# A half chunk of keys in four quarters of the array: head-mixed attention in front of two gated layers

## The chip, the cores and the metric

The kernel runs on one core of one Trainium2 chip. The metric is the time of the device in microseconds (us) for one execution; a time that is given for a kernel is the median of several runs. The profile is of one execution, taken by the hardware profiler, and has its own time.

## The reference

Attention with 4 batches, 12 heads, 448 positions and 64 numbers a head, in which the heads are mixed before and after the softmax, and behind it two gated layers:

```python
scores = scale * np.matmul(q, k.transpose(0, 1, 3, 2))
scores = np.einsum('bhij,hg->bgij', scores, w_pre)      # first mixing
scores = scores - np.max(scores, axis=-1, keepdims=True)
attn = np.exp(scores)
attn = attn / (np.sum(attn, axis=-1, keepdims=True) + 1e-09)
attn = np.einsum('bhij,hg->bgij', attn, w_post)         # second mixing
out = np.matmul(attn, v)
...
gate = 1.0 / (1.0 + np.exp(-(x @ w_gate)))              # 1792 x 768, d_ff 1536
x = gate * (x @ w_val) @ w_out
h = x @ w_in                                            # d_ff 2048
return h * (1.0 / (1.0 + np.exp(-1.702 * h))) @ w_out2
```

All of it is float32.

## The kernel before, in words

The program has two parts. `attention` does the attention and writes its result to `xd` in memory; `Ffn` does the two layers from `xd`. The change touches `attention` and one helper of `Ffn` (`prepare`) that works beside it.

In `attention` the 448 queries of a batch are cut into four units of 120, 120, 120 and 88 queries, 16 units in all. For each of the six pairs of heads of a batch, q and k are loaded as rows (`load_pair`, tile `nat`), turned on TensorE against an identity (`turn`, L300: four transposes of 112 rows for a part, k and q apart; q of the first batch comes in two halves), and copied into `kq` by ScalarE or VectorE. `qk` (L340) makes the scores of a unit. A DMA per half group (`relayout`, `gt<-sc`, L359) puts five queries x twelve heads on 60 partitions; two such blocks lie in the two row halves of the array. A unit of 120 queries has 6 groups of 20 queries, one of 88 has 2 of 20 and 3 of 16: 92 groups. Per group come `premix` (L368, the first mixing, in four quarters of 64 x 64 of the array), maximum and exponent, `norm` (its last step on GpSimd, L393, makes `w`, the second mixing's weights divided by the sums) and `postmix` (L415, the second mixing).

The 448 keys are seven chunks of 64. `postmix` lays chunk c on partitions 0 to 63 and chunk c + 4 on 64 to 127 of its result. The fourth chunk has no partner: its two matmuls per row half both go to the left column half, and the other 64 partitions hold zeros. `post_out` copies the result to `at`; `av` (L436) multiplies it with v: for each of 12 heads 4 matmuls over all 128 partitions, two heads abreast in the two column halves. The fourth of the four is half zeros: `vt[64:, :, NC - 1]` is set to 0 once. A float32 matmul is two records in the trace, so a group of `postmix` has 56 records (28 matmuls) and a unit of `av` 96 (48 matmuls). `vt` is one buffer: `load_v` (L326) brings v of the next batch in two large DMAs once the last `av` of the batch has read it.

The order on every engine is written out: each piece of work is added to a list with the engines it may use, and `PLAN` is a text of tokens, one per piece, that fixes the order in which pieces are issued, their engine (S for ScalarE, V for VectorE, P for GpSimd, Y for SyncE) and their PSUM banks. Each engine works its pieces off in that order and waits for what a piece needs. SyncE issues nearly all DMAs. Beside the attention run 28 pieces of weight conversion for `Ffn` (`prepare`: a load into `pf`, steps on ScalarE and VectorE, a write of `pc` to `kept`), load and write on SyncE.

Of the kernel before, what the change touches and what calls it, by code (L numbers as in the profile page):

```python
# [9 lines left out]
F32 = mybir.dt.float32  # L10
# [64 lines left out]
0Y 3:0 1S 6:1 7V 1cY cS 1f:2 f:3 1oY 8 oS pS dY 4V 5 20:45 10S 11Y gV h r:6 sV 1gS 1h 1dS 1pS 2Y qY 21S u:7 vV  # L75
t i:1 eY jS k w 13:0 1r:3 16:2 14S 17V 22V 1i:6 1jS 23:41 1sS 1k 2c:75 15 25S 12S 24V 9:6 aS 18 2eS 1u:1 29:04
1t 1vV 1w 2dS 2bS 26:23 28S 1qY 2f:51 2aV 27V dd de 19:7 l:0 1x:4 2gS 2hV mV 1aV 1b b 4z:32 51V df:5 x:1 yV
1eS n dgV dh 1yS 1z 58:76 5aV 52:20 59S 54S 5e:75 2i 2j 2k:04 2l 53S 2v 50S di:2 2w 38 39 5gS 2n 3l 3m 3y 3z
4b 5fS z 2x:63 2y 2m 1l:5 1mV 1n 2z 2o 55:70 56S 4c 1fg 30 5b:15 5dV 3a:64 3b djS dk 31 32 2p 3c 3n:75 3d 3e
5cS 3f 2q 33 34 2r 57S 40:32 41 42 3o 3g 3h 3p 2s:64 3q 43 2tV 3r 3i:10 44 45 4d:37 4e 2uS 4g 4o 3jV 3kV 4f 4h  # L80
4i 4j 5h 7w:56 7yV 46 3s 5i 7xS 35:24 36S 3t 82:31 dl 7z:70 80V 37V 83S 84S 4k 88:56 89S 5u 85:23 87V 4l:17 3u
81V 3v:45 4mV 3wS 4nV 3xS 5j:30 47 48:17 5k 4p 5v 5m 86S 8b:45 49S 4aV 5l 5n 5w:21 4q:7 8cV 5x 5y 1fw 4r 67 68
5o 6k 5p 5q 8aV 4s dn:3 1fx 5z 60 69:40 4u:2 4v 6l 6x 6y 7a 7b 1fh 4w 8dV dt 5r:65 61 4tV 1fy 1fz 6a 8e 6b 6c
6d doS 6m:17 4xS dp 62 5sS 5tS 1g0 6z:40 7c:32 8f 8r 8s 6n 6p 6e 6o 6q 63 70 6f 71 72 73 1g2 at:65 avS auV
64:17 7d 7e 74 6g 94 6h:46 6r 6iS 7f 7g 6jV 8g:05 95 dv:3 dm 6s 6t 65S b2:46 66S dwV 8h 6u:21 7h 7i 9h 1g1 9i
8i 6vS az:70 b3V 7j 1g3 b1S dx 8j 7k:43 8k 75 76 e9 6wV aw:21 7lV du 7mS b0S 8t:05 1g4 1g5 8u q2 axS ayS 1g6
eh b4S dq:4 77:37 drS 96:21 97 9u 9v 1g8 8v 9j:60 9k e1 78S 79S 7n:3 a7 8l 7o 7p 9l 8w 8x 98 99 b8:76 9a b5:52
a8 9b e2 b6S dy:1 9m ds b9V 9n 9c 9o baV ea eb:4 ecS 8m b7V 8n dzS e0 ed 1g9 1ga 9w:75 7r:6 7s 7t 9x 9z 9y 7qV
q3 8y 8z ei qa 7uS ej:0 bb bc 9d e3:2 ekV a9:14 a0 bo a1 8o:73 1gb 1gc 90 e4S 8pS q4:6 a2 1ge 8qS 9p e6:5 1g7
ee:7 efS aa el 9e:03 1fi ab q5S e7V e8 9q 9fS em:5 enS e5 ep:12 eg 9gV ac ev:70 eqS q6 exS eo 4yP ad ae qc:3  # L90
bp q7:1 9r:60 ewS af qi qdV erS 9sS 9tV a3 a4:54 c1 c2 ag q8V ah:72 aiS 1gf qe f1:60 a5V a6S ey:35 ajV q9
f4:72 f0S f3V ce 1gg 1gh ezS f5S f2S 1gi f6V cf cr cs 1fj 1gk es:10 etS bd:45 91:37 7vP be bg bq:62 1gj euS bf
bh 1gd f7 f8 92V c3:10 93V c4 c5 cg:43 ak:7 al ch ci c6 c7 am cj ck cl ao:5 ap cm fk fl fx anV br c8 cn 1gl
1gm bi bj bs fy bt bk aq ct:14 bu bv c9 ca f9:03 ga gb gn go arV h0 bl:76 qy 1gn cu cv cw fa fc cb:25 cx h1
bmV fb fd cy 1go ccV co:14 cdS bnV cpS ho:07 cqV 1gq 1fk hu:35 hqS i0:21 qb hx:64 hwV i2V bw bx i1S hr:75
i3:21 hpV cz d0 htS fe i4V hsV fm:05 fn hyS fz:62 asP hzS ff fg hvS fp by:43 i5S g0 gc:71 fo g2 fq fr bzV c0V
d1:05 r6 g1 gp:64 d2V gq gd d3S d4:3 1gr gf 1gs d5 d6 d8:5 d9 gr ge fs ft g3 gg gh gs gt gu i6 i7 da d7V 1gt
# [60 lines left out]
def attention(tc, q, k, v, w_pre, w_post, xd, after):  # L158
# [20 lines left out]
    EB = 5  # L179
    KB = NP + 2  # L180
    SB = 4
    NPRE = 6

    units = []
    groups = []
# [25 lines left out]
    with ExitStack() as ctx:  # L211
# [66 lines left out]
        psq = {}  # L278

        def load_pair(b, p, i, queue):  # L280

# [1489 lines left out]
```

## Time and profile before

| | |
|---|---|
| times of three runs | 1284.29, 1292.66, 1293.9 us; median 1292.66 |
| profiled execution | 1287.18 us, its span 1285.4 us |
| TensorE busy | 1247.9 us (97% of the span) |
| VectorE, ScalarE, GpSimd busy | 1004.2 us, 819.4 us, 57.8 us |
| mean granted clock of TensorE | 0.990 |

The span is what the trace covers, from the first to the last instruction; the profiled execution took 1.8 us more. TensorE counts as busy while a matmul is in flight, and matmuls overlap. Attention fills the span up to about 395 us; from 700 us on TensorE is busy at 98% and over with the layers. A granted clock of 1.00 is 2.4 GHz, 0.5 is 1.2 GHz, and a mean in between says for how much of a stretch each held.

### The profile page before, as it was taken

Reading aid. Unit: us, or ns where it says so; the run is one execution under the profiler, and the core shown is the slowest. Engines: PE = TensorE matmul, PEld = TensorE weight load, DVE = VectorE, ACT = ScalarE, POOL = GpSimd, SP = SyncE. Lnnn points to the kernel's source line nnn. Section 1 sums busy time; section 2 is a strip of 40 time slices with the busy share of each in tenths; the row PEclk is TensorE's granted clock in tenths of the full one; section 3 lists DMA queues with packets and bytes.
Section 4 is the critical chain, followed back from the end, with each engine's and each line's share of the span. In section 5 each row is a group of like instructions: output and inputs, shape, how many; then the busy total and the mean of one; then the engine's idle time right before and its main releaser. Section 6 shows DMA issues by size and latency. Waiting matters only on the chain.

```text
span 1285.4 us, 33205 instructions
## 1 busy us (share of the span) xinstructions
PE 1247.9 (97%) x12770; PEld 1115.6 (87%) x12770; DVE 1004.2 (78%) x2142; ACT 819.4 (64%) x1968; POOL 57.8 (4%) x138
## 2 busy tenths in 40 slices
PE   7999899899999999999999999999999999999998
PEld 5677676678679899989999999999999999999998
DVE  6787587698876999988889898878866795565863
ACT  3877587688884767667567666656665455565442
POOL 3111011010110000000000000000000000000000
PEclk9998899899999999999999999999999999999999
DMA  6877777677776665489976445894626872125653
GB/s 165 229 206 235 184 204 229 179 226 225 222 261 207 200 214 171 130 268 326 326 266 218 142 155 195 287 304 158 220 73 172 284 271 81 50 62 156 213 156 123
DMA packets 216111, 256.87 MB, mean 200 GB/s; under 512 B 60413, under 2 KB 202513, under 8 KB 215953
## 3 DMA queue, kind: packets, MB, share of 16 engines
q1 hardware_dynamic: 208944, 249.32, 61.7%
q0 software_dynamic: 1344, 4.05, 1.0%
q10 hardware_dynamic: 5664, 1.38, 0.5%
q8 instruction: 101, 1.65, 0.5%
q14 instruction: 58, 0.47, 0.1%
HBM read 160.18 MB, written 55.97 MB: 168 GB/s over the span
## 4 chain that ended last, share of the span: by engine, by line
PE 54%; DVE 7%; DMA 2%; issue 2%; ACT 1%; SPq 0%; DVEq 0%; ACTq 0%
PE pq L1155 27%; PE po L1642 14%; PE py L1100 13%; DVE xy L1137 1%; DVE w L1022 1%; DVE xy L1293 1%; DMA xy<-kept 1%; DVE s L1293 1%; DVE wc L894 1%; DMA sb<-xy 1%; DVE s L1164 0%; DMA wf<-sb 0%; ACT xy L1136 0%; DVE wt L1293 0%; DVE wc L893 0%
## 5 line engine op out<-in xcount | busy, mean ns | idle before, releaser
L1155 PE MATMUL pq<-xy,w 128*128 128x448 f32 x2394 | 482.1, 362 | 1.6 <-ACT s L1204 0.8
L1155 PEld LDWEIGHTS pq<-xy,w 128*128 128x128 f32 x2394 | 447.7, 187 | 35.3 <-ACT s L1204 2.3
L1642 PE MATMUL po<-wf,xy 128*128 128x384 f32 x1176 | 204.7, 335 | 2.6 <-DMA wf<-sb 2.6
L1642 PEld LDWEIGHTS po<-wf,xy 128*128 128x128 f32 x1176 | 203.9, 188 | 3.2 <-ACT xy L1088 2.3
L1100 PE MATMUL py<-xy,w 128*128 128x448 f32 x864 | 173.7, 362 | 1.5 <-DVE xy L1086 1.4
L1100 PEld LDWEIGHTS py<-xy,w 128*128 128x128 f32 x864 | 161.9, 187 | 12.9 <-DVE xy L1086 2.1
L380 ACT ACTIVATE ex<-bank,st 128x448 f32<-128x448 f32 x184 | 115.8, 635 | 29.3 <-DVE st L374 27.7
L415 PEld LDWEIGHTS bank<-w,ex 60*64 60x64 f32 (+1 forms) x5152 | 101.7, 136 | 35.3 <-issue 28.3
L374 DVE TENSOR_REDUCE st<-bank 128x1 f32<-128x448 f32 x184 | 107.3, 617 | 29.1 <-PE bank L368 25.8
L1136 ACT CAST xy<-xy 128x384 fp32r<-128x384 f32 (+2 forms) x212 | 89.1, 457 | 57.9 <-DVE xy L1293 55.0
L415 PE MATMUL bank<-w,ex 60*64 60x60 f32 (+2 forms) x5152 | 104.8, 222 | 11.4 <-issue 10.8
L1137 DVE TENSOR_TENSOR xy<-xy 128x384 fp32r<-128x384 f32 (+2 forms) x212 | 95.7, 486 | 22.4 <-ACT xy L1136 22.3
L1293 DVE TENSOR_TENSOR xy<-xy 128x384 f32<-128x384 f32 (+2 forms) x184 | 90.9, 512 | 15.8 <-DMA xy<-xd 7.0
L368 PE MATMUL bank<-gt,wpre 64*64 64x448 f32 (+2 forms) x736 | 96.3, 578 | 3.2 <-ACT at L304 2.9
L1016 ACT CAST w<-xy 128x384 fp32r<-128x384 f32 x110 | 55.1, 510 | 53.1 <-DVE xy L1293 29.2
L436 PEld LDWEIGHTS bank<-at,vt 128*64 128x64 f32 x1536 | 74.6, 138 | 14.2 <-ACT at L304 3.5
L340 PE MATMUL bank<-kq 64*120 64x448 f32 (+1 forms) x576 | 77.7, 396 | 6.1 <-issue 5.3
L1022 DVE TENSOR_TENSOR w<-wt,w 128x384 fp32r<-128x384 f32 x108 | 59.2, 553 | 27.6 <-ACT w L1016 27.6
L436 PE MATMUL bank<-at,vt 128*64 128x120 f32 (+1 forms) x1536 | 79.7, 262 | 0.7 <-ACT at L304 0.4
L890 ACT ACTIVATE wc<-ws 128x384 f32<-128x384 f32 x108 | 59.8, 554 | 30.1 <-DMA ws<-in_moe_w_in_dram 20.5
L340 PEld LDWEIGHTS bank<-kq 64*120 64x120 f32 (+1 forms) x576 | 52.5, 181 | 23.8 <-issue 7.1
L1164 DVE TENSOR_TENSOR s<-s,pq 128x448 f32<-128x448 f32 x80 | 49.4, 619 | 28.4 <-PE pq L1155 28.4
(98 smaller groups left out, 1534.6 us busy)
## 6 DMA issues: line engine op xcount, KB each, us to landing
gt<-sc SPq DMA_DIRECT2D x160, 210.0 KB
wf<-sb SPq DMA_DIRECT2D x64, 384.0 KB
xy<-kept SPq DMA_DIRECT2D x60, 384.0 KB
ws<-in_moe_w_out_dram SPq DMA_DIRECT2D x56, 384.0 KB
kept<-wc SPq DMA_DIRECT2D x108, 192.0 KB
ws<-kept SPq DMA_DIRECT2D x46, 384.0 KB
sb<-xy SPq DMA_DIRECT2D x32, 384.0 KB
ws<-in_moe_w_in_dram SPq DMA_DIRECT2D x32, 384.0 KB
```

The costliest lines, as they stand in the source:

```text
L340: nc.tensor.matmul(ps[a][:n, :S], w[at_, qp, 1, i0:i0 + n], w[at_, kp, 0], start=(i == 0), stop=(i == 2), tile_position=(a * 64, 0))
L368: nc.tensor.matmul(pre[s][row][64 * col:64 * col + 64, :S], wpre[r], x[r, col], start=True, stop=True, tile_position=(64 * row, 64 * col))
L374: nc.vector.tensor_reduce(out=rs[s][:, j:j + 1], in_=pre[s][j][:, :S], axis=AX.X, op=ALU.max, negate=True)
L380: nc.scalar.activation(ex[s][:, j], pre[s][j][:, :S], AF.Exp, bias=st[:, j:j + 1], scale=1.0, accum_out=st[:, 2 + j:3 + j])
L415: nc.tensor.matmul(ps[row][64 * k:64 * k + 64, c, :, j * m:(j + 1) * m], e[r, j, (c + k * NC) * 64:(c + k * NC + 1) * 64], w[r, j, :, i0:i ...
L436: nc.tensor.matmul(psv[u, half][a * 64:a * 64 + 64, r, :n], vt[:, g, c, :], at[:, c, g, :n], start=(c == 0), stop=(c == NC - 1), tile_posi ...
L1100: self.nc.tensor.matmul(acc[hb][:, :self.S], st, act[k0 + kc][hb][:, ap], start=(k0 + kc == 0 and part == 0 and ap == 0), stop=(k0 + kc == ...
L1136: self.nc.scalar.copy(dst[:, 0], src)
L1137: self.after(n, lambda: self.nc.vector.tensor_tensor(out=dst[:, 1], in0=src, in1=dst[:, 0].bitcast(F32), op=ALU.subtract))
L1155: nc.tensor.matmul(x, st, A[p][c][:, ap], start=(first and c + part + ap == 0), stop=(c == self.KG - 1 and part == 1), skip_group_check=no ...
L1293: self.nc.vector.tensor_tensor(out=dst, in0=x, in1=y, op=op)
L1642: nc.tensor.matmul(acc[:, :PW], x[:, part], w[:, wp], start=(start and part == 0 and wp == 0), stop=(stop and part == 1), skip_group_check ...
```

## The change

Second mixing: the fourth chunk's first block of queries (j = 0) goes to the left column half and its second (j = 1) to the right one, so its four matmuls use four different quarters. Multiplication with v: `av` now does chunks 0 to 2 alone, over 128 partitions, as before; the fourth chunk is done by `remains` in quarters of 64 x 64. Rows 0 to 63 hold the first half of every block's queries and rows 64 to 127 the second, so v of that chunk is loaded to both row halves. The two row halves must not write to one bank together: `remains` runs twice, in the second pass with the banks swapped, and a memset of one element on GpSimd (`between`) stands between the passes, for which the second waits. Both banks of a unit stay open until both passes are done.

Transposes: k lies on partitions 0 to 63 and q on 64 to 127, seven transposes of 64 rows each, and from the second batch on k and q are turned side by side in the two row halves. v comes in nine DMAs a batch (four of three heads for chunks 0 to 3, four for 4 to 6, one for the copy of chunk 3). Loads and writes of the weight conversion may be issued by GpSimd: 12 of 28 loads and 24 of 28 writes are. `PLAN` is another one; its first line and the core of the rest:

```diff
-0Y 3:0 1S 6:1 7V 1cY cS 1f:2 f:3 1oY 8 oS pS dY 4V 5 20:45 10S 11Y gV h r:6 sV 1gS 1h 1dS 1pS 2Y qY 21S u:7 vV
...
+0S 1Y 3:0 4V 10Y 11Y cS f:1 6:2 dY 5 7V 8 13:3 14V 1oS 2Y 1qS gS h oY pY 1pS i:4 jV k 1cY 1dY 20:56 16:7 23:02
...
-            return ((0, NJ), (0, NJ)) if b else ((0, NJ), (0, NJ // 2), (NJ // 2, NJ))
+            return ((0, S), (0, S)) if b else ((0, S), (0, S // 2), (S // 2, S))
...
+            for _, _, out, x, one, at_ in sorted(todo, key=lambda y: y[:2]):
+                nc.tensor.transpose(out, x, one, tile_position=(at_, 0))
...
+        def load_v(b, x, h0):
+
+            row, to, key, n = ((0, 0, 0, NC), (1, 0, NC, NC - 1), (1, NC - 1, NC - 1, 1))[x]
+            h = slice(h0, H if x == 2 else h0 + VH)
+            nc.sync.dma_start(vt[64 * row:64 * row + 64, h, to:to + n],
+                              v[b, h].rearrange("h (m g) d -> m h g d", g=HC)[:, :, key:key + n])
...
-                    for k in range(1 + (c + NC < HC)):
+                    for k in (0, 1) if c < NC - 1 else (j,):
+                        key = (c + k * NC if c < NC - 1 else c) * 64
...
+        def between(u):
+
+            y = nc.gpsimd.memset(mark, 0.0)
+            after_(y, order[u])
+            order[u] = y
+
+        def remains(u, x):
+
+            c = NC - 1
+            first = True
+            for r in range(NP // 2):
+                for row in range(2):
+                    half = row ^ x
+                    p = slice(64 * row, 64 * row + 64)
+                    for r0, count, rows in blocks[u]:
+                        m = rows // 2
+                        cols = lambda y: y[:, r0:r0 + count * rows].rearrange("p (g i) -> p g i", i=rows)[:, :, row * m:row * m + m]
+                        for a in range(2):
+                            g = 2 * (half * NP // 2 + r) + a
+                            y = nc.tensor.matmul(cols(psv[u, half][a * 64:a * 64 + 64, r]), vt[p, g, c, :], cols(at[p, c, g]),
+                                                 start=False, stop=True, tile_position=(64 * row, 64 * a),
+                                                 skip_group_check=True)
...
-            x = work.add(t, dict(SP=(540, 1800)), load, takes=("pf",), since=t, load=1300)
+            x = work.add(t, dict(SP=(540, 1800), POOL=(900, 2400)), load, takes=("pf",), since=t, load=1300)
```

TensorE, the multiplication with v of one unit of 120 queries. Before, the first of its two runs of 24 matmuls over 128 partitions (`x24`; a row is an operation, its tiles and the size of its result):

```order
L368 MATMUL bank_254<-gt_281,wpre 64x448
L368 MATMUL bank_250<-gt_281,wpre 64x448
...
L436 MATMUL bank_258<-at,vt 64x120 x24
L340 MATMUL bank_274<-kq 88x448
L340 MATMUL bank_270<-kq 88x448
```

Now, of the unit at the same place, both banks side by side, the first pass of `remains` (L485), a run of `av` (L457) while GpSimd sets its mark, and the start of the second pass:

```order
L457 MATMUL bank_262<-at,vt 64x120 x6
L457 MATMUL bank_270<-at,vt 64x120 x18
L389 MATMUL bank_250<-gt_279,wpre 64x448
L389 MATMUL bank_246<-gt_279,wpre 64x448
...
L485 MATMUL bank_262<-at,vt 64x12x5 x2
L485 MATMUL bank_270<-at,vt 64x12x5 x2
...
L457 MATMUL bank_262<-at,vt 64x120 x12
L485 MATMUL bank_270<-at,vt 64x12x5 x2
L485 MATMUL bank_262<-at,vt 64x12x5 x2
```

One run of equal matmuls a bank has become runs of two kinds that alternate. Counted over all of attention, TensorE's order changes between whole array, row halves, column halves and quarters 149 times before and 181 times now.

SyncE, where v of the second batch is loaded. Before, two DMAs, and behind them the relayouts and loads that wait their turn:

```order
L932 DMA pf<-in_moe_w_val_dram 128x3x256
L359 DMA gt_279<-sc 120x1x448
L326 DMA vt<-in_v_dram 64x12x256
L326 DMA vt<-in_v_dram 64x12x192
L359 DMA gt_280<-sc 120x1x448
L291 DMA nat<-in_k_dram 112x4x64 x2
```

Now nine, without another DMA between them:

```order
L997 DMA pf<-in_moe_w_val_dram 128x3x256
L347 DMA vt<-in_v_dram 64x3x256 x4
L347 DMA vt<-in_v_dram 64x3x192 x4
L347 DMA vt<-in_v_dram 64x12x64
L380 DMA gt_280<-sc 120x1x448 x2
L380 DMA gt_281<-sc 120x1x448
```

The same bytes, and 192 KB more, go out in smaller steps, and stay one block in SyncE's order.

GpSimd, in the second batch. Before, its order holds the `w` of each group and a store of `xo` now and then:

```order
L393 TENSOR_TENSOR w_3803<-wpost,st 128x120
L453 DMA xd_58<-xo 768x1x120
L393 TENSOR_TENSOR w_3929<-wpost,st 128x120
L393 TENSOR_TENSOR w_4055<-wpost,st 128x120
L393 TENSOR_TENSOR w_4097<-wpost,st 128x120
```

Now loads and writes of the weight conversion and the marks stand among them:

```order
L414 TENSOR_TENSOR w_3297<-wpost,st 128x120
L468 MEMSET mark 1x1
L997 DMA pf<-in_moe_w_val_dram 128x3x256
L414 TENSOR_TENSOR w_3472<-wpost,st 128x120
L508 DMA xd_58<-xo 768x1x120
L1006 DMA kept_67<-pc 128x384
L414 TENSOR_TENSOR w_3502<-wpost,st 128x120
```

A `w` there is now queued behind DMAs that themselves wait for a buffer or a result.

## Rows read from the trace of the kernel before

**Rows 1.** Stretches: busy us and instructions per engine, PEclk, DMA share, GB/s.
```profile
150.00:200.00 50.00, 49.91 (x1158) 38.51 (x1152) 42.69 (x90) 41.57 (x116) 6.63 (x15) 1.00 0.72 211
```

**Rows 2.** Timeline of TensorE: second mixing; start us, us, line, shapes, records.
```profile
64.62 1.15 PE L415 MATMUL bank<-w,ex 60*64 60x60 f32 x56
...
111.43 2.95 PE L415 MATMUL bank<-w,ex 60*64 60x60 f32 x168
...
385.21 1.14 PE L415 MATMUL bank<-w,ex 60*64 60x48 f32 x56
386.27 2.68 PE L1100 MATMUL pg<-xy,w 128*128 128x448 f32 x12
```

**Rows 3.** Timeline of TensorE: multiplication with v, units of 120 and 88 queries.
```profile
104.81 5.14 PE L436 MATMUL bank<-at,vt 128*64 128x120 f32 x96
...
388.88 3.86 PE L436 MATMUL bank<-at,vt 128*64 128x88 f32 x96
```

**Rows 4.** Timeline of TensorE: transposes, one part alone and two together.
```profile
69.53 0.60 PE L300 MATMUL bank<-ident,nat 112*128 112x112 f32 x4
...
88.18 0.98 PE L300 MATMUL bank<-ident,nat 112*128 112x112 f32 x8
```

**Rows 5.** Waits of TensorE, 0 to 400 us: total us, times, longest.
```profile
PE bank L415 <- issue: 10.8, 8, 3.3
PE bank L340 <- issue: 5.3, 2, 4.6
```

**Rows 6.** Timeline of TensorE: three idle times (in brackets), in batches 2 to 4.
```profile
143.25 3.34 PE L340 MATMUL bank<-kq 64*120 64x448 f32 x16 [4.59 <-issue]
...
237.55 1.11 PE L415 MATMUL bank<-w,ex 60*64 60x60 f32 x23 [3.29 <-issue]
...
324.34 1.67 PE L415 MATMUL bank<-w,ex 60*64 60x60 f32 x86 [1.47 <-issue]
```

**Rows 7.** Stretches of 5 us around idle times; columns as in Rows 1.
```profile
95.00:100.00 5.00, 2.70 (x36) 1.95 (x39) 2.21 (x5) 4.03 (x9) 0.00 (x0) 0.70 0.54 175
100.00:105.00 5.00, 5.00 (x69) 3.63 (x63) 2.81 (x5) 1.38 (x5) 0.00 (x0) 0.62 0.80 253
...
140.00:145.00 5.00, 1.75 (x10) 1.75 (x11) 0.35 (x1) 0.53 (x1) 0.00 (x0) 0.64 0.99 197
145.00:150.00 5.00, 5.00 (x99) 3.08 (x100) 2.77 (x6) 1.82 (x5) 0.39 (x1) 0.68 0.11 32
...
235.00:240.00 5.00, 2.45 (x31) 2.18 (x32) 1.12 (x2) 1.97 (x5) 0.00 (x0) 0.69 0.88 243
240.00:245.00 5.00, 5.00 (x82) 3.00 (x78) 2.40 (x4) 1.63 (x4) 0.00 (x0) 0.62 0.70 201
```

**Rows 8.** Timeline of SyncE's queue: start us, us to issue, line, count.
```profile
131.09 1.35 SPq L326 DMA_DIRECT2D vt<-in_v_dram  x2
...
135.36 2.46 SPq L359 DMA_DIRECT2D gt<-sc  x1
...
148.74 0.40 SPq L932 DMA_DIRECT2D pf<-in_moe_w_val_dram  x1
```

**Rows 9.** DMA: a queue (packets, MB, share), and v's issues (count, KB each).
```profile
q8 instruction: 101, 1.65, 0.5%
...
vt<-in_v_dram SPq DMA_DIRECT2D x4, 768.0 KB
...
vt<-in_v_dram SPq DMA_DIRECT2D x4, 576.0 KB
```

**Rows 10.** Timelines of ScalarE and TensorE: an idle time at 95 us.
```profile
95.96 0.55 ACT L890 ACTIVATE pc<-pf 128x384 f32<-128x384 f32 x1 [3.24 <-DMA kept<-pc]
...
97.45 2.19 PE L368 MATMUL bank<-gt,wpre 64*64 64x448 f32 x8 [2.30 <-ACT at L304]
```

**Rows 11.** SyncE's waits for the conversion; GpSimd's DMA issues (count, busy, mean ns).
```profile
SPq L932 <- DVE pc L896: 39.4, 20, 6.4
...
L453 POOL DMA_DIRECT2D xd<-xo x12 | 9.7, 817 | 18.0 <-ACT xo L304 17.5
```

More of the change, by code (lines that the diff above doesn't have):

```diff
@@ L154 @@
+1hc 1o5 1o7 1ol 1ha 1o8 1om 1o9 1oa 1ob 1oc 1oe 1on 1mz 1of 1ns 1hd 1he 1oo 1op 1hfV 1hgV 1oq 1o6 1or 1hh 1hx
+1od
 """
@@ L560, in add_av @@
             late = first[u] + last[u] + 1 >= TAIL
+            full = [[], []]
+            for c in range(NC - 1):
+                for half in range(2):
+                    x = work.add(t + c * AVH // 2 + half, dict(PE=(5.2 * n, 5.2 * n + 180)), lambda e, half=half, c=c: av(u, half, c),
+                                 needs=out[u] + vready[b] if c + half == 0 else [],
+                                 behind=full[half][-1:] or full[0][-1:], banks=1 if c == 0 else 0, late=late, mode="columns", size=24)
+                    full[half].append(x)
+            ends = []
+            for y in range(2):
+                x = work.add(t + 2 * AVH + y, dict(PE=(360, 540)), lambda e, y=y: remains(u, y), needs=ends[-1:], behind=[full[1][0]],
+                             mode="quad", size=48 * len(blocks[u]))
+                ends.append(x)
+                if y == 0:
+                    ends.append(work.add(t + 2 * AVH, dict(POOL=(80, 250)), lambda e: between(u), needs=[x]))
+            done = work.add(t + 2 * AVH + 2, dict(none=(0, 0)), lambda e: None, needs=[x, full[0][-1], full[1][-1]],
+                            gives=("a", "v") if u % nu == nu - 1 else ("a",))
             prev = []
-            x = None
             for half in range(2):
-                for some in AVS:
-                    done = half == 1 and some is AVS[-1]
-                    y = work.add(t + half * AVH + some[0] * AVR, dict(PE=(7 * n * len(some), 7 * n * len(some) + 180)),
-                                 lambda e, half=half, some=some: av(u, half, some), needs=[] if x else out[u] + [vready[b, c] for c in range(2)],
-                                 behind=[x] if x else [], banks=0 if some[0] else 1, late=late, mode="columns", size=32 * len(some),
-                                 gives=() if not done else ("a", "v") if u % nu == nu - 1 else ("a",))
-                    x = y
-                    if some[0] == 0:
-                        holds = x
                 prev = [work.add(t + half * AVH + 2410, dict(ACT=(585, 840), DVE=(560, 720)), lambda e, half=half: av_out(u, half, e),
-                                 needs=[x] + prev, takes=() if half else ("xo",), frees=((holds, 0),))]
+                                 needs=[x, full[half][-1]] + prev, takes=() if half else ("xo",), frees=((full[half][0], 0),))]
                 if not late:
@@ L597, in attention @@
                 if ci == 0:
[L598 to L601 removed]
+                    vready[b] = []
+                    for c in range(3):
+                        for h0 in range(0, H, H if c == 2 else VH):
+                            vready[b].append(work.add((first[u] + 2 + 2 * c) * STEP + 1113 + 300 * h0, dict(SP=(650, 850)),
+                                                      load=790 if c == 2 else (2650, 2070)[c] * VH // H,
+                                                      emit=lambda e, b=b, c=c, h0=h0: load_v(b, c, h0), takes=() if vready[b] else ("v",),
+                                                      behind=vready[b][-1:], since=0 if b else THIRD))
                 add_av(u)
```

292 lines of the change are left out of this document (156 added, 136 removed).

## The prediction

> **What bounds the kernel now.** I read the busy times by stage first, then TensorE's timeline in attention, then what its idle time waited for. Attention takes the first 395 us, and in it TensorE is the engine that is never far from full: 49.9 of 50 us in an undisturbed stretch, with VectorE at 42.7 and ScalarE at 41.6 [rows 1]. So TensorE time saved in attention comes off the end, as far as the other two, 85% and 83% busy there, keep up. The layers behind it have the same order on every engine in both kernels; they start when attention ends, and I move them as a block.
>
> Attention is not always undisturbed. The reader is to see two kinds of loss. First, TensorE stood idle 10.8 + 5.3 us in waits for nothing that the profile shows [rows 5], the largest of them three of 4.59, 3.29 and 1.47 us, each a few us after v of the next batch was issued [rows 6, 8]. After the first two the granted clock falls: in the four 5 us stretches that hold them it is 0.64, 0.68, 0.69 and 0.62 [rows 7], so (0.36 + 0.32) x 5 = 3.4 us and (0.31 + 0.38) x 5 = 3.45 us at 1.2 GHz are lost besides. Second, at 95 us ScalarE waited 3.24 us for a write of converted weights to land, TensorE then 2.30 us for ScalarE [rows 10], and the clock was 0.70 and 0.62 [rows 7], another 3.4 us.
>
> **The change part by part.** The sum is made against the profiled execution, 1287.2 us (span 1285.4).
>
> Second mixing. Three groups on end take 2.95 us and one takes 1.15 [rows 2], so one more group costs 0.90 us. Its 56 records are 48 four abreast and 8 two abreast: 12 + 4 = 16 passes, 56 ns each. The last 8 now go four abreast: 2 passes less, 0.113 us, in 92 groups **-10.4 us**. The number of matmuls stays.
>
> Multiplication with v. A unit of 120 queries takes 5.14 us, one of 88 takes 3.86 us [rows 3]. The fourth chunk is a quarter, 1.285 and 0.965 us, and goes. In its place a unit of 120 gets 24 matmuls in quarters, 48 records of 60 columns, the shape of the second mixing: 12 passes of 56 ns, 0.67 us. That is -0.61 us in 12 units, **-7.3 us**. A unit of 88 has two blocks, so 48 matmuls, 96 records, of 20 and 24 columns. Are these shorter? A group with 48 columns took 1.14 us, one with 60 took 1.15 [rows 2]: a pass does not get shorter with fewer columns. So 24 passes, 1.34 us, +0.38 us in 4 units, **+1.5 us**. If the quarters ran only two abreast, it would be +0.06 and +1.73 us instead, in all +7.6 where I have -5.8: that bound is a rival below.
>
> Changes of shape. TensorE's order goes between whole array, halves and quarters 32 times more often. Their price: the lone group at 385.21 us is followed by the next matmul 1.06 us later [rows 2], 0.16 us more than a group among its like. 32 x 0.16 = **+5.1 us**. Bounds: nothing, if the replaced work would have paid it; and 32 x 0.22 = 7.0 by the transposes (0.60 us for 4, 0.98 for 8 [rows 4]: 0.095 each and 0.22 around them).
>
> Transposes. A pair from the second batch on took 0.98 us at best; now seven passes of 64 rows, k and q abreast. With 95 ns a pass, as before (a turned tile still has 128 columns), 0.885 us: -1.7 us in 18 pairs. With 56 ns, as a pass of 64 columns, 0.61 us: -6.7 us. The first batch has 15 transposes a pair where it had 8, alone in their halves: 42 more, +2.4 to +4.0 us. Together -4.3 to +2.3; I take **0**, in between.
>
> The mark. GpSimd's memset stands between the two passes, but TensorE's order has a run of other matmuls between the two passes in every unit. I cost it at nothing. If GpSimd is just issuing a DMA, 0.82 us [rows 11], a unit could wait about that.
>
> v in small DMAs. Before, 768 + 576 KB (1.38 MB) are issued in 1.35 us [rows 8, 9]; at the 197 GB/s of that stretch [rows 7] they take 7.0 us, so 5.6 us of it stand in the engines once the issue is done. TensorE's instructions come by DMA as well, 101 packets of 16 KB [rows 9]; my reading is that one of these got stuck behind v. Now 1.57 MB, 8.0 us, go out in nine steps. At 0.68 us a step, as v's took, that lasts 6.1 us and leaves 1.9 us standing; at 0.40 us, as the smallest issue of the rows [rows 8], 3.6 and 4.4 us. So what an instruction packet meets shrinks by a fifth to two thirds. The three stalls with their clock cost 4.59 + 3.29 + 1.47 + 6.85 = 16.2 us; I take half, **-8 us**, between 3.4 and 10.7; the ends are -16.2 if no stall is left, and +3 if 1 us more of transfer in three batches is paid in full. SyncE is blocked for 6 us instead of 1.35, but the relayout behind v waited 2.46 us for room anyway [rows 8].
>
> Conversion on GpSimd. 24 of 28 writes no longer stand behind loads of q and k on SyncE. The loss at 95 us, 2.3 + 3.4 = 5.7 us, was of that kind; half of it, **-2.9 us**, between 0 and -5.7. What it puts in front of `w` on GpSimd is the second rival.
>
> Sum: -10.4 - 7.3 + 1.5 + 5.1 + 0 - 8 - 2.9 = -22.0, 1265.2 us for an execution like the profiled one. The median of three runs stood 5.5 us over that one and its lowest 2.9 below; I add half of the 5.5: **1268 us**.
>
> **The rivals.** *The stalls stay.* v still goes out in one block, and its bytes are more. If a packet of instructions waits for the whole block, or for something else, the last two terms fall away: 1265.2 + 10.9 + 2.7 = 1279 us. For it speaks that of the 16.1 us of such waits [rows 5] 6.7 came away from v; against it, that the longest came behind v. The Trainium skill, "DMA: Bandwidth & Descriptors", section "Queues, rings and completion order", says that an engine takes turns between its queues packet by packet; by that rule v could not hold the instructions up for us, and cutting it would give nothing, which is this rival's time. The trace speaks against the rule as I read it, with 4.59 us idle, but shows no packet's wait directly. Chance 0.24.
>
> *GpSimd holds up `w`.* SyncE waited 20 times, 39.4 us in all and 6.4 at the longest, to issue a load of the conversion, because its buffer was still in use [rows 11]. Twelve such loads now wait on GpSimd, with the `w` of the next groups and the marks behind them, and `postmix` needs `w`. For it: that place and those waits. Against it: `w` is made a few us ahead, and the new order may place loads later. A stall of 2.3 us with its 3.4 us of clock costs 5.7; seven of them add 40 us to the forecast, 1308 us. It decides against the kernel from the seventh on; with three it takes the gain to 1285. Chance 0.09.
>
> *The quarters run two abreast* in the multiplication with v, because its two row halves write to two banks in turn or its columns lie five by five. Then the change does not do there what it says: 13.4 us more, 1281 us. Against it: the second mixing runs four abreast. Chance 0.07.
>
> *All of it works.* No stall behind v or the conversion, transposes at 56 ns, no price for the changes of shape: -10.4 - 7.3 + 1.5 - 4.3 - 16.2 - 5.7 = -42.4, with the 2.7 about 1247 us. Chance 0.12.
>
> **How the numbers follow.** The forecast has 0.48 and a spread of about 10 us to either side, since a new order has new places where TensorE waits and the three times shown lie 9.6 us apart. 1% is 13 us, about what can be told from no change: faster is below 1279.7, slower above 1305.6. Faster: 0.45 of the forecast's 0.48, half of the first rival, a little of the third, all of the last: 0.72. Slower: nearly all of the second, 0.08. Within 1%: 0.20. The range, 1245 to 1287 us, takes in the last rival and the first with some spread and leaves out the slow one.
>
> **What would show it.** The second mixing: a group among its like at 0.79 us where it was 0.90. v: `av` and `remains` together near 4.5 us in a unit of 120 and 4.2 in one of 88; more says two abreast or dear changes of shape. Transposes: seven pairs in 0.6 or 0.9 us. v's DMAs: no idle time of TensorE over 3 us in the 10 us behind them, and PEclk at 1.00 there; SyncE's nine issues spread over 4 to 6 us. GpSimd: no idle time of TensorE in L437 put down to `w`, nor in L485 put down to the mark. Attention should end near 373 us. I would be wrong if it ended there and the layers took longer, or if TensorE's busy time fell by some 15 us and its idle time rose by as much.

## The result, and the profile after

The changed kernel takes 1307.27 us (median of 4 runs, 1301.08 to 1312.39) against 1293.28 us before in the same session: ratio 1.0113, 95% interval 1.0075 to 1.0150. It is 14 us slower where 25 us less was forecast; the time lies outside the range. The profiled execution has a span of 1310.7 us.

The loss is in attention. I count it up to the first `pq` matmul, which starts at 416.8 us before and at 435.5 us after, 18.7 us later. (The first matmuls of the layers, `pg` and `pv`, stand in front of it in both, so this mark lies behind the 395 us of the prediction.) From there to the end it was 868.6 us before, 875.2 us after, and 869.3 to 875.6 us in all the kernels below, whose work there is the same: the 6.6 us are the scatter of single executions.

TensorE's timeline after, as in [rows 2 to 4]: start, us, line, shapes, records.
```profile
92.40 0.99 PE L437 MATMUL bank<-w,ex 60*64 60x60 f32 x56
...
229.57 1.59 PE L457 MATMUL bank<-at,vt 128*64 128x88 f32 x36
231.09 0.92 PE L485 MATMUL bank<-at,vt 64*64 64x20 f32 x48
...
350.23 1.81 PE L437 MATMUL bank<-w,ex 60*64 60x60 f32 x112
...
370.85 2.07 PE L457 MATMUL bank<-at,vt 128*64 128x120 f32 x36
372.85 0.58 PE L485 MATMUL bank<-at,vt 64*64 64x60 f32 x24
373.36 0.84 PE L457 MATMUL bank<-at,vt 128*64 128x120 f32 x12
```
Two groups on end take 0.82 us more than one (0.79 forecast, 0.90 before). In `av` three chunks of half a unit take 2.00 us from start to start (370.85 to 372.85) and 24 records in quarters 0.51 us: about 5.0 us for a unit of 120, where 4.5 was forecast. For 88 queries it is 2 x (1.52 + 0.85) = 4.7 us, with 4.2 forecast and 3.86 before (3.79 from start to start).

The waits of TensorE after, 0 to 400 us, as in [rows 5]: total us, times, longest.
```profile
PE bank L437 <- issue: 12.9, 9, 4.5
PE bank L320 <- DMA nat<-in_k_dram: 4.8, 1, 4.8
PE bank L320 <- DMA nat<-in_q_dram: 4.2, 2, 3.1
PE bank L361 <- ACT ex L401: 3.7, 5, 2.3
PE bank L389 <- DMA gt<-sc: 2.9, 2, 2.5
PE bank L389 <- ACT at L323: 2.7, 1, 2.7
PE bank L457 <- issue: 2.4, 2, 1.7
```
The waits with no visible releaser ("issue") are 16.7 us in all rows, as before (16.5); those for ScalarE went from 3.3 to 11.7 us, and all waits from 27.9 to 44.4 us.

The idle times, as in [rows 6, 10]: TensorE, then ScalarE.
```profile
173.80 1.42 PE L361 MATMUL bank<-kq 64*88 64x448 f32 x5 [2.35 <-ACT ex L401]
...
198.74 1.33 PE L361 MATMUL bank<-kq 64*120 64x448 f32 x6 [1.84 <-ACT sc L323]
...
246.24 1.64 PE L437 MATMUL bank<-w,ex 60*64 60x60 f32 x50 [4.54 <-issue]
```
```profile
172.15 0.54 ACT L955 ACTIVATE pc<-pf 128x384 f32<-128x384 f32 x1 [3.10 <-DMA kept<-pc]
...
197.29 0.54 ACT L955 ACTIVATE pc<-pf 128x384 f32<-128x384 f32 x1 [2.38 <-DMA kept<-pc]
```
ScalarE's first step of a conversion waits for a write to land, and TensorE then waits for what ScalarE has behind it. Before, there was one such place [rows 10].

SyncE's queue and the stretches of 5 us at the third batch of v, as in [rows 7, 8], then GpSimd's DMA issues, as in [rows 11].
```profile
234.23 9.90 SPq L347 DMA_DIRECT2D vt<-in_v_dram  x9
244.26 5.86 SPq L380 DMA_DIRECT2D gt<-sc  x3
```
```profile
240.00:245.00 5.00, 1.70 (x21) 1.13 (x18) 2.79 (x8) 2.15 (x7) 0.00 (x0) 0.94 1.04 210
245.00:250.00 5.00, 3.76 (x63) 2.31 (x64) 1.07 (x2) 1.47 (x3) 2.05 (x4) 0.50 0.98 182
```
```profile
L1006 POOL DMA_DIRECT2D kept<-pc x24 | 14.1, 587 | 20.0 <-DVE pc L961 18.8 <-issue 0.4 <-DVE pc L958 0.2
```
One long stall behind v is left of three, with a clock of 0.50 after it. SyncE's nine issues took 9.90 us here, where 4 to 6 was forecast.

### The profile page after: what moved, and what is told of

The parts are those of the page before. It is cut to its first block, busy times and chain, and to the rows that moved or that the text cites. A ratio compares the mean times of both kernels' runs of the same rounds, so it can differ in the third digit from the quotient of the medians.

```text
span 1310.7 us, 34684 instructions
## 1 busy us (share of the span) xinstructions
PE 1253.2 (96%) x13496; PEld 1104.4 (84%) x13496; DVE 1001.0 (76%) x2139; ACT 822.8 (63%) x1971; POOL 80.9 (6%) x188
## 4 chain that ended last, share of the span: by engine, by line
PE 55%; DVE 5%; DMA 2%; issue 1%; ACT 1%; SPq 0%; DVEq 0%; ACTq 0%
PE pq L1224 27%; PE po L1711 16%; PE py L1169 12%; DMA xy<-kept 1%; DVE w L1091 1%; DVE xy L1206 1%; DVE s L1233 1%; DVE xy L1362 1%; DMA sb<-xy 0%; DVE s L1362 0%; DMA wf<-sb 0%; DVE wc L959 0%; ACT xy L1205 0%; DVE wc L958 0%; DVE wc L961 0%
## 5 line engine op out<-in xcount | busy, mean ns | idle before, releaser
L1711 PE MATMUL po<-wf,xy 128*128 128x384 f32 x1176 | 208.5, 339 | 2.6 <-ACT xy L1205 2.0
L1711 PEld LDWEIGHTS po<-wf,xy 128*128 128x128 f32 x1176 | 207.6, 189 | 3.3 <-ACT xy L1157 2.3
L401 ACT ACTIVATE ex<-bank,st 128x448 f32<-128x448 f32 x184 | 115.7, 633 | 29.8 <-DVE st L395 28.3
L437 PEld LDWEIGHTS bank<-w,ex 60*64 60x64 f32 (+1 forms) x5152 | 93.7, 138 | 47.1 <-issue 32.0
L437 PE MATMUL bank<-w,ex 60*64 60x60 f32 (+2 forms) x5152 | 99.9, 224 | 18.7 <-issue 13.9
L389 PE MATMUL bank<-gt,wpre 64*64 64x448 f32 x736 | 98.3, 586 | 5.6 <-DMA gt<-sc 2.9
L361 PE MATMUL bank<-kq 64*120 64x448 f32 (+1 forms) x576 | 89.2, 409 | 8.1 <-ACT ex L401 3.7
L457 PEld LDWEIGHTS bank<-at,vt 128*64 128x64 f32 x1152 | 55.8, 137 | 14.7 <-issue 6.6
L323 ACT COPY at<-bank 128x480 f32<-128x480 f32 (+1 forms) x104 | 54.0, 560 | 20.6 <-PE bank L437 20.5
```

What stands on the lines that cost most here:

```text
L361: nc.tensor.matmul(ps[a][:n, :S], w[at_, qp, 1, i0:i0 + n], w[at_, kp, 0], start=(i == 0), stop=(i == 2), tile_position=(a * 64, 0))
L389: nc.tensor.matmul(pre[s][row][64 * col:64 * col + 64, :S], wpre[r], x[r, col], start=True, stop=True, tile_position=(64 * row, 64 * col))
L401: nc.scalar.activation(ex[s][:, j], pre[s][j][:, :S], AF.Exp, bias=st[:, j:j + 1], scale=1.0, accum_out=st[:, 2 + j:3 + j])
L437: nc.tensor.matmul(ps[row][64 * k:64 * k + 64, c, :, j * m:(j + 1) * m], e[r, j, key:key + 64], w[r, j, :, i0:i0 + m], start=True, stop=Tr ...
L1711: nc.tensor.matmul(acc[:, :PW], x[:, part], w[:, wp], start=(start and part == 0 and wp == 0), stop=(stop and part == 1), skip_group_check ...
```

## The experiments

Each was timed in five rounds beside the kernel before; us are medians, ratios are to the kernel before with their 95% interval.

**Parts of the change, one at a time, in the kernel before.** First the fourth chunk on quarters.
```diff
-                    for k in range(1 + (c + NC < HC)):
+                    for k in (0, 1) if c + NC < HC else (j,):
...
```


> The kernel before with one part of the change: the fourth chunk of the second mixing goes to the column half of its j, so its four multiplications run on four quarters at once instead of on two, twice over. The product with v is as before, so half of that chunk's share is left out of the result. Theory A (TensorE's own work is the bound, and the prediction's term for the second mixing is right): one 58 ns step less for each of 184 calls of 28 multiplications, 10 to 11 us less, ratio 0.992 (0.990 to 0.994). Rival B (the step is given back by the evictions behind it, which free the banks no sooner): 0 to -3 us, ratio 0.998 to 1.001.

Measured 1292.02 us, 1.0006 (0.9973 to 1.0039): nothing that can be told, 3.5 us at most. TensorE's work fell by 6.3 us, and its idle time rose by 6.1 (table below); its waits with no visible releaser went from 16.5 to 20.6 us, most of them in `postmix`:
```profile
PE bank L415 <- issue: 16.2, 9, 5.4
```
Theory A falls.

> The kernel before with one part of the change: the same 12 loads and 24 writes of the weight conversion as in the changed kernel are issued on GpSimd instead of SyncE, each at the place it has in the kernel before. Theory A (GpSimd's transfers land late, 6.6 us and 4.5 us after issue, and ScalarE's first step of a conversion waits for them in front of its copies and exponentials): slower by 5 to 15 us, ratio 1.004 to 1.012, with ScalarE's waits for these transfers up from 3 us to 15 us or more. Rival B (the new stalls of the changed kernel come from its new order, not from the queue): within 3 us of the kernel before. Rival C (the prediction's own term): 3 us faster.

The edit is `(e or self.nc.sync).dma_start(...)` for the 36 transfers, with the engine from the table. Measured 1302.40 us, 1.0078 (1.0045 to 1.0110): 10 us slower, theory A. ScalarE's timeline, then TensorE's:
```profile
145.81 0.55 ACT L887 ACTIVATE pc<-pf 128x384 f32<-128x384 f32 x1 [6.81 <-DMA kept<-pc]
...
214.38 0.54 ACT L887 ACTIVATE pc<-pf 128x384 f32<-128x384 f32 x1 [5.63 <-DMA pf<-in_moe_w_val_dram]
```
```profile
147.30 2.59 PE L337 MATMUL bank<-kq 64*120 64x448 f32 x11 [2.12 <-ACT at L301]
...
216.12 0.29 PE L412 MATMUL bank<-w,ex 60*64 60x60 f32 x2 [3.00 <-ACT ex L377]
```
ScalarE waits 14.1 us for these transfers (5.8 before), and TensorE waits behind it.

v split:
```diff
-            nc.sync.dma_start(vt[64 * x:64 * x + 64, :, :c.stop - c.start],
-                              v[b].rearrange("h (m g) d -> m h g d", g=HC)[:, :, c])
+            for h in range(0, H, 3):
+                nc.sync.dma_start(vt[64 * x:64 * x + 64, h:h + 3, :c.stop - c.start],
+                                  v[b, h:h + 3].rearrange("h (m g) d -> m h g d", g=HC)[:, :, c])
```


> The kernel before with one part of the change: each of the two loads of v is issued as four of three heads, one right behind the other on SyncE, in the place of the large one. The transfers in front and behind keep their places. Theory A (the block is one transfer of 64 partitions whose packets hold back the instructions' packets; pieces back to back carry the same packets): the three idle times of 4.59, 3.29 and 1.47 us stay, within 2 us of the kernel before. Rival B (smaller transfers let the instructions through): the idle times fall by half, 8 us faster, ratio 0.994.

Measured 1281.20 us, **0.9899** (0.9861 to 0.9938): 12.5 us less, rival B and more. Its waits of TensorE, 0 to 400 us:
```profile
PE bank L416 <- issue: 7.9, 8, 1.5
...
PE pg L1101 <- issue: 2.0, 1, 2.0
```
The longest in `postmix` is 1.5 us, where [rows 5] has 3.3 us, and 4.6 us in `qk`. About half of what its profile gains in attention is the clock: 6.8 us at half clock instead of 23.9 (table below). The same with six pieces (`range(0, H, 2)`):

> The kernel before with v's two loads each issued as six transfers of two heads, one right behind the other on SyncE (the run with four of three heads gave 0.990). Theory A (the smaller the pieces, the shorter an instruction's packet waits): the same or a little less, ratio 0.986 to 0.990. Rival B (the gain comes from the time that SyncE takes between the issues, which spreads the block; with twelve issues the relayout behind them comes later and TensorE waits for it): ratio 0.990 to 0.996.

Measured 1283.57 us, 0.9911 (0.9879 to 0.9944): no better than four. Quarters and split together:

> The kernel before with two parts of the change: the fourth chunk of the second mixing on quarters, as in the run with that alone (ratio 1.0006; half of that chunk's share is left out of the result), and v in four transfers of three heads each, as in the run with that alone (ratio 0.990). Theory A (the step that the quarters save was taken back by TensorE's wait for its own instructions, whose fetch v's large transfers hold up; with v in pieces the fetch keeps up): 7 to 11 us less than the split alone, ratio 0.982 to 0.985. Rival B (the saved step is given back whatever v does, by the evictions or by a fetch that has its own pace): the same as the split alone, ratio 0.988 to 0.992.

Measured 1280.51 us, 0.9895 (0.9859 to 0.9930): the same as the split alone, rival B. That leaves the copies or the pace of the fetch for the quarters' saving.

**Parts undone in the changed kernel.**

> The changed kernel, in which nobody waits for the conversion's transfers during the attention: all 28 loads and 28 writes are still issued in the same places on the same queues, but the conversion's steps read a small constant tile and the writes send that tile, so the converted weights are left out of the result. Theory A (ScalarE's 24 us of waiting for these transfers, behind which its copies and exponentials stand, is what cost the changed kernel its gain): 12 to 20 us less than the changed kernel, about 1290 us, ratio 0.997 to the kernel before, and the idle times of TensorE at 171, 197, 276 and 361 us with their stretches at half clock gone. Rival B (instruction fetch and the longer work of TensorE took the gain): at most 5 us less than the changed kernel, ratio 1.007 or more.

Measured 1300.74 us, 1.0051 (1.0021 to 1.0080): 6.5 us less, between the two; idle time stayed at 39.4 us (41.7 in the changed kernel), with other places in the place of the four.

> The changed kernel with one part undone: the 12 loads and 24 writes of the conversion that went to GpSimd are issued on SyncE again, at the same places. Theory A (the queue costs here what it cost alone in the kernel before, about 9 us up to the end of the attention): 7 to 11 us less than the changed kernel, ratio to the kernel before 1.003 to 1.006, ScalarE's waits for these transfers down from 24 us to under 10. Rival B (SyncE, with 36 issues more, hands out the relayout's and v's transfers later, and TensorE waits for those): within 3 us of the changed kernel.

Measured 1303.70 us, 1.0093 (1.0065 to 1.0121): 3.6 us less, rival B as far as the intervals tell. ScalarE's waits for these transfers are 20.8 us still:
```profile
ACT pc L951 <- DMA kept<-pc: 10.5, 5, 4.3
...
ACT pc L951 <- DMA pf<-in_moe_w_val_dram: 9.1, 4, 2.9
```
So here the wait goes with the places that the new order gives to loads, steps and writes, more than with the queue.

> The changed kernel without the quarter passes that multiply the fourth chunk with v, and without the mark between them; that chunk's share is left out of the result. Theory A (the passes are 17.5 us of TensorE's own work, with changes of tile shape about them, and TensorE is the bound): 18 to 22 us less than the changed kernel, ratio to the kernel before 0.994 to 0.997. Rival B (what TensorE saves it waits for its instructions or for other engines): 5 to 10 us less, ratio 1.003 to 1.007.

The edit is a `return` at the head of `remains` and `between`. Measured 1306.97 us, 1.0096 (1.0061 to 1.0130): no difference in the runs. In the profiles TensorE's work fell by 14.3 us, its idle time rose by 6.1, and attention ended 8.0 us sooner; but the profiled execution was the shortest of its kernel (1298.60 us) and that of the changed kernel its longest (1312.39), and the medians, 0.3 us apart, don't show that. Theory A falls.

> The changed kernel with one part undone: each of v's two large pieces is one transfer of all twelve heads again, at the place of its first piece. Theory A (the split saves as much here as alone in the kernel before, where it was 12.5 us): 10 to 14 us more than the changed kernel, ratio to the kernel before 1.019 to 1.022. Rival B (in the changed order the split saves little, since the stall of 4.54 us behind the third batch of v is still there): within 4 us of the changed kernel, ratio 1.008 to 1.014.

Measured 1317.26 us, 1.0159 (1.0112 to 1.0205): 10 us more by the medians, 6 by the ratios, between the theories.

> The changed kernel with one part undone: q and k are loaded in 112 partitions and turned by four or eight transposes of 112 x 112 in a row, as before. Theory A (the transposes side by side save what their quicker passes save, 7 us of TensorE's work, less 4 us at the start, where loads of 56 partitions are issued at 0.82 us instead of 0.31 us each): within 4 us of the changed kernel, ratio to the kernel before 1.008 to 1.015. Rival B (the loads in more and smaller pieces delay the instruction fetch and the relayout all through the first 250 us): 5 to 10 us less than the changed kernel, ratio 1.003 to 1.007.

Measured 1306.01 us, 1.0086 (1.0056 to 1.0117): theory A; transposes are worth nothing here that can be told.

> The changed kernel with its first part undone: the second mixing's fourth chunk on two quarters as before, its product with v at full height in the places of the quarter passes, no mark. Theory A (TensorE's work is covered by what it waits for, as in the runs with the quarters alone and without the quarter passes): within 4 us of the changed kernel, ratio to the kernel before 1.008 to 1.015. Rival B (TensorE's work decides: 10.7 us more in the second mixing, 1 to 2 us less in the product with v): 8 to 10 us more than the changed kernel, ratio 1.018 or so.

The edit also leaves out v's third load, the copy of the fourth chunk. Measured 1310.09 us, 1.0124 (1.0090 to 1.0158): theory A; the quarters, with all that they need, are worth nothing that can be told.

**The order alone.** All five parts undone, the table `PLAN` kept but for the engine of the conversion's 36 transfers, which is SyncE again; the fourth chunk's product with v stands where the quarter passes stood:
```diff
 def remains(u, x):
+    return av(u, x, NC - 1)
```


> The changed kernel with every part undone but its order: transposes and their loads as before, the second mixing's fourth chunk on two quarters and its product with v at full height (in the places of the quarter passes), v in two transfers, the conversion on SyncE. The work is that of the kernel before; the table that sets the order, and the product with v chunk by chunk, are the changed kernel's. Theory A (the parts undone singly gave back 2 to 8 us of 14, so the rest lies in the new order, whose waits on transfers and other engines are its own): slower than before by 15 to 25 us, ratio 1.012 to 1.020. Rival B (the order is as good as the old one, and the loss is the sum of transposes, quarter passes and GpSimd's queue): within 5 us of the kernel before, ratio 0.997 to 1.004.

Measured 1310.34 us, **1.0105** (1.0070 to 1.0140): a loss as large as that of the changed kernel, with the work of the kernel before. The ratio lies under theory A's 1.012, its interval reaches into it, and rival B is out. With v split added:

> The kernel with the changed kernel's order alone (ratio 1.0105), with v in pieces of three heads added, at the places that the changed order gives them. Theory A (order and split add: 1.0105 and 0.990): ratio 0.998 to 1.003. Rival B (in the new order the split is worth half, as the changed kernel with v whole showed, 1.0159 against 1.0113): ratio 1.004 to 1.008.

Measured 1293.22 us, 1.0020 (0.9995 to 1.0045): order and split add up, theory A.

**Where saved work goes.** The copies behind the second mixing halved (`at[:, :, :H // 2, ...]`):

> The kernel before with v in four pieces (ratio 0.990), in which the copies behind the second mixing, on ScalarE and VectorE, carry six of the twelve heads; the other six heads' weights are left out of the result. It takes about 184 times 0.25 us from the two engines, some 23 us from each. Theory A (in the stretches without stalls VectorE is busy 88 and ScalarE 86 of 100, and the three engines wait for each other in turn, so that shorter copies pay): 5 to 12 us less than the split alone, ratio 0.981 to 0.986. Rival B (TensorE alone is the bound): the same as the split alone, 0.988 to 0.992.

Measured 1283.22 us, 0.9946 (0.9920 to 0.9971): no gain. The ratio is above both ranges; theory A falls, though TensorE's work isn't the bound either.

> As the run with v split and half copies, with the fourth chunk of the second mixing on quarters besides (what these leave out is left out here too). Theory A (the copies and exponentials took what the quarters saved): with shorter copies the quarters pay 6 to 10 us, ratio 0.005 to 0.008 under that of the run with half copies alone. Rival B (the quarters' saving goes to TensorE's wait for its instructions, 9.9 us with the split alone and 12.6 us with quarters besides): within 0.003 of it.

Measured 1280.14 us, 0.9923 (0.9895 to 0.9951): 0.0023 under the run before, rival B; TensorE's waits without a releaser are 18.2 us, where they were 12.3 without the quarters.

> The changed kernel with the copies behind the second mixing cut to six of twelve heads (the other six heads are left out of the result). Theory A (the new order loses by waits between TensorE, ScalarE and VectorE): 10 to 20 us less than the changed kernel, ratio to the kernel before 0.996 to 1.004. Rival B (it loses by transfers, instruction fetch and changes of tile shape, which shorter copies leave as they are): at most 5 us less, ratio 1.007 or more.

Measured 1305.80 us, 1.0135 (1.0098 to 1.0173): rival B. Then fewer transfers: no loads of raw weights, and `range(0, 3, 3)` in the split of v. The conversion's steps read a constant tile and its writes send that tile, so ScalarE waits neither for a load nor for a write to land.

> The kernel before with v split (ratio 0.990), and with fewer transfers in the attention: the 28 loads of raw weights (384 KB each) and three of the four pieces of each of v's two loads are not issued, so the conversion works on a constant and nine heads of v are zero in the result. About 15 MB of the 85 MB that are moved up to 400 us are gone; the work of TensorE, ScalarE and VectorE is the same. Theory A (TensorE's instructions come late because their packets stand behind others): its waits for instructions fall from 9.9 us to under 5, ratio 0.980 to 0.986. Rival B (the fetch has a pace of its own, or TensorE's work is the bound here): waits for instructions of 8 us or more, ratio 0.987 to 0.992.

Measured 1268.84 us, **0.9810** (0.9771 to 0.9850). Theory A. TensorE's waits of this kind, and three stretches of 100 us (engines as in [rows 1]; the last three numbers are PEclk, DMA share, GB/s):
```profile
PE bank L414 <- issue: 3.2, 2, 2.1
```
```profile
0.00:100.00 100.00, 91.74 (x1676) 64.62 (x1678) 76.76 (x168) 68.01 (x180) 23.16 (x56) 1.00 0.66 186
100.00:200.00 100.00, 98.35 (x2364) 78.35 (x2360) 83.34 (x183) 82.40 (x232) 14.09 (x32) 1.00 0.61 187
200.00:300.00 100.00, 99.66 (x2531) 78.33 (x2532) 87.34 (x190) 83.67 (x236) 13.19 (x31) 1.00 0.58 181
```
The same stretches of the run with v split and all transfers:
```profile
100.00:200.00 100.00, 98.01 (x2354) 76.67 (x2346) 82.63 (x178) 80.53 (x227) 12.59 (x29) 1.00 0.81 226
200.00:300.00 100.00, 97.12 (x2373) 75.42 (x2373) 86.16 (x188) 82.26 (x229) 13.74 (x31) 1.00 0.77 233
```
With a DMA share of 0.6 in place of 0.8, the waits without a releaser fall from 9.9 to 3.2 us, which is most of the fall of idle time from 16.7 to 9.1. ScalarE waits for no load here either (3.6 us with all transfers), so not all of the gain need be the instructions'.

> As the run with fewer transfers, with the fourth chunk of the second mixing on quarters besides (half of that chunk's share is left out too). Theory A (the quarters' saving was taken by late instructions, 12.6 us of waits with v split and 17.5 us with half copies besides, and those came late behind other transfers): with fewer transfers the quarters pay, 6 to 10 us, ratio 0.005 to 0.008 under that of the run without them. Rival B (in the stretches of the second mixing the instructions are used up faster than they are fetched, whatever else is moved): within 0.003 of that run, with TensorE's waits for instructions longer by 3 us or more.

Measured 1263.53 us, 0.9784 (0.9745 to 0.9823):
```profile
PE bank L414 <- issue: 3.3, 3, 1.4
```
The waits don't grow this time (3.2 and 3.3 us), and attention ends 5.1 us sooner (393.6 and 388.5 us), most of the 6.5 us by which TensorE's work fell. The runs are 5.3 us apart by the medians and 0.0026, 3.4 us, by the ratios, which is inside rival B's 0.003; the two intervals overlap. So the waits and the profile speak for theory A, and the times alone don't decide.

For the table I took TensorE's records up to the first `pq`: work is the time from one record's start to the next one's, at most to its own end, halved where the clock is half; idle is the rest; all in us.

| kernel | attention ends | work | idle | at half clock |
|---|---|---|---|---|
| before | 416.8 | 377.9 | 23.7 | 23.9 |
| changed | 435.5 | 375.2 | 41.7 | 30.7 |
| quarters alone | 417.9 | 371.6 | 29.8 | 27.3 |
| v split alone | 400.6 | 375.9 | 16.7 | 6.8 |
| quarters and split | 404.7 | 372.4 | 21.0 | 13.7 |
| changed, no quarter passes | 427.5 | 360.9 | 47.8 | 30.7 |
| order alone | 434.7 | 387.4 | 33.2 | 20.5 |
| order with split | 423.2 | 388.2 | 25.4 | 10.2 |
| split, fewer transfers | 393.6 | 378.2 | 9.1 | 3.4 |
| the same with quarters | 388.5 | 371.7 | 10.7 | 3.4 |

Each row is one execution: before, v split alone and the one without quarter passes are 6 to 8 us under the median of their kernel, the changed one 5 us over it. So a difference of some us between two rows is not shown by them; the times of the runs decide.

## Why the prediction was wrong

**The step that failed first: a new order at the price of its changes of shape.** I gave the new order +5.1 us and a spread of 10, and took the waits of the old order over. Alone it costs 13.6 us by its ratio, about the whole distance between the kernels; with the split and nothing else the changed order comes out even (1.0020). From there to the changed kernel (1.0113) are 12 us more, which came with the transposes, the quarters and GpSimd's queue on top of the new order; undone one at a time these gave back 4 us at most, so how they share the 12 us is open. In its profile, with the same matmuls as before, TensorE's work is 9.5 us longer, of it `qk` 5.5 (72.1 to 77.6) and `premix` 4.1 (78.8 to 82.9), and its idle time 9.5 us longer. TensorE's order changes shape 179 times in it, 30 times more than before (I had counted 32 for the changed kernel); at my 0.16 us that makes 4.8 of the 9.5 us. The longer idle time isn't in the waits with no visible releaser, which are 16.5 us in both: waits for ScalarE rose from 3.3 to 6.5, for VectorE from 0.7 to 2.0, for the relayout `gt` from 0.3 to 3.7 us:
```profile
PE bank L427 <- issue: 15.1, 7, 4.6
...
PE bank L379 <- DMA gt<-sc: 3.7, 2, 2.2
PE bank L427 <- ACT ex L391: 2.5, 3, 1.9
PE bank L351 <- ACT ex L391: 2.2, 4, 1.1
```
Which of its places cost what was not separated.

**"TensorE time saved in attention comes off the end."** This failed too. I read it from one stretch with 49.9 of 50 us [rows 1]. The second mixing's term was right in kind as work, and two thirds of it came: -10.4 forecast, -7.1 measured in the kernel before (93.4 to 86.3 us), as one group more now costs 0.82 us and not 0.79. As time it was nothing that can be told, alone, with v split, or undone in the changed kernel. Leaving out the quarter passes showed the same. Shorter copies of ScalarE and VectorE brought nothing either, so those two aren't the bound in its place. What paid was fewer transfers; with them the quarters gave 3 to 5 us, with half copies some 3 us, and in both cases the intervals overlap.

What took the saved work is TensorE's wait for its own instructions, which come in packets of 16 KB beside the other transfers [rows 9]. The packets and instructions that the traces hold show it. The kernel before has 25,833 matmuls, weight loads and other instructions on TensorE and 101 packets, 256 instructions to a packet. Between 10 and 400 us of all twenty traces TensorE has 151 idle times of over 0.7 us with no visible releaser. Counted along its order, every one of them stands in front of instruction 193 or 194 of a block of 256 (counted from 0), where 2 of its 94 other idle times of that length do; and each ends 1.2 to 1.8 us after such a packet has landed. In the kernel before the packet inside the stall of 4.59 us runs from 140.15 to 141.77 us, 1.5 us after TensorE stopped, and in the changed kernel one runs from 243.3 to 244.6 us inside the stall of 4.54 us. A packet takes about 1.0 us (median) in the kernel before and with fewer transfers alike, but it starts 1.7 us after TensorE passed the last such place in the one and 1.0 us in the other (medians). So what differs between these two traces is when a packet starts, and not how long it takes. The second mixing uses its instructions up quickest, and the quicker it is, the sooner TensorE stands: with the quarters these waits rose from 16.5 to 20.6 us, from 9.9 to 12.6 with v split and from 12.3 to 18.2 with half copies besides, and only with fewer transfers not at all.

The Trainium skill, "Runtime: NRT & Kernel Launch", section "Instruction fetch mechanics", says that the crossing from one 16 KiB block of instructions to the next is mostly hidden. By that the waits at such crossings should be small whatever else is moved; here they were 16.5 us before and 3.2 us with fewer transfers, so for small matmuls beside busy queues the measurement decides against it.

**v in small DMAs**, -8 us between -3.4 and -10.7: the mechanism was right and worth more, 12.5 us alone (the far end was 16.2) and 11 us in the new order (1.0105 to 1.0020). In the changed kernel 6 to 10 us. The rival in which the stalls stay is out as to the split, whose pieces shorten them; but in the changed kernel the sum of these waits did stay (16.7 us, 16.5 before), at other places of its order. By the Trainium skill, "DMA: Bandwidth & Descriptors", section "Queues, rings and completion order", an engine takes turns between its queues packet by packet. The rule that I drew from it, that v could not hold the instructions up, doesn't give this: cutting v alone gave 12.5 us.

**Conversion on GpSimd**, -2.9 us: wrong in sign. It cost 10 us in the old order; undone in the changed kernel it gave back 3.6 us, which can't be told from nothing. I looked at what the writes stand behind on SyncE, and not at when they land: on GpSimd's queue a write landed 4.5 us after its issue and a load 6.6 us (medians after), and ScalarE's copies and exponentials stand behind the step that waits for them. No row gives SyncE's times to landing beside these; what is shown is that ScalarE's waits rose from 5.8 to 14.1 us with the queue alone. The rival with GpSimd's queue gave 1308 us, near the measured time, but by another way: waits of TensorE for `w` are 1.4 us in all, and for the mark there are none.

**The product with v**, -5.8 us: mis-sized. From start to start 5.07 to 5.0 us in 12 units and 3.79 to 4.7 us in 4 make about +3 us; summed over all its records the work rose by 1.3 us (77.4 to 78.7). Its passes were right: four records start every 58 ns, so the rival with two abreast is out. The rest are changes of shape, some 0.16 us for each of a unit's two runs in quarters (0.51 us less six passes), 5 us in all. These I had priced apart, at +5.1, so the two terms together (-0.7) fell short by 2 to 4 us. In time it didn't matter, as the kernel with the old second mixing shows.

**Transposes** at 0 and **the mark** at 0 stand: undoing the first made no difference that can be told, and nothing waits for the second. The layers behind attention moved as a block, as assumed.

**A better kernel.** The kernel before with v in four pieces, and nothing else of the change, takes 1281.20 us and beats both: 12.5 us under before, some 26 us under the changed kernel.

## What to carry to other kernels

A stretch in which an engine is full shows that it can be the bound there, not that its saved time comes off the end: before counting on it, take the work away in an experiment and see whether idle time takes its place. Where a profile names no releaser for an engine's waits, number the engine's instructions: here all of them stood at one place of every 256, which made them waits for the next packet of instructions. A change that comes with a new order of the work is two changes; run the new order with the old work, since its waits can't be read from the old profile. Ask of each transfer moved to another queue when it lands and what the engine that waits for it has behind that wait.

## What the runs showed of the hardware

- TensorE's waits without a visible releaser stand at one place of every 256 of its instructions (151 of 151 in twenty traces), and end 1.2 to 1.8 us after a 16 KB packet of instructions has landed.
- They go with the other transfers: 16.5 us before, 9.9 with v in pieces, 3.2 with 15 MB less besides, in kernels with the same matmuls.
- A pass of four quarters takes the same 58 ns with 20 columns as with 60, by the starts of the records within a run. With the changes of shape at its ends, a run of 48 records of 20 and 24 columns takes 0.72 to 0.85 us from start to start, one of 24 records of 60 columns 0.40 to 0.51.
- In the first 30 us SyncE took 0.84 us (median) to issue a load of q in 56 partitions, and 0.46 us for one of as many bytes in 112 partitions. (The 0.31 us in an expectation above is the shortest of the latter.) After and then before, with shortest, median and longest in ns (two of each row are loads of twice the bytes):
```profile
L306 SPq DMA_DIRECT2D nat<-in_q_dram x18: 624/837/1044, 0.8 to 21.6; - x18
```
```profile
L291 SPq DMA_DIRECT2D nat<-in_q_dram x14: 312/456/490, 5.3 to 20.0; - x14
```
